# A state-space convolution's phase reduced inside its matmul, a first transform stage in 64x64 tiles, and another order of issue

## The chip, the cores and the metric

The kernel runs on one core of a Trainium2 chip. The metric is the device time of one execution in microseconds (us), median of the runs shown. A core has a matmul engine (TensorE, PE in the profile; its weight loads are PEld), three engines that work on data in SBUF and PSUM (VectorE: DVE, ScalarE: ACT, GpSimd: POOL), and a queue engine (SyncE: SP) that issues most transfers. Each engine takes its instructions in the order of the program.

## The reference

Two blocks with residuals, on one sequence of L = 2048 positions and D = 512 channels. The change lies in the first block, an S4D convolution, and in the start of the second, a gated MLP.

```python
dt = exp(log_dt);  A = -exp(log_A_real) + 1j * A_imag;  C = (C_real + 1j * C_imag) * dt[:, None]
P = exp((A * dt[:, None])[:, :, None] * pos)           # 512 channels x 128 states x 2048 positions
K = 2.0 * einsum("dn,dnl->dl", C, P).real              # a filter for each channel
y = irfft(rfft(u_t, 2 * L) * rfft(K, 2 * L), 2 * L)[:, :, :L]
h = x + (y + u * D_skip)                               # u = layernorm(x)
# second block, on layernorm(h):
z = gelu(x @ w_in);  z1 = z[..., :896];  z2 = layernorm(z[..., 896:])
out = h + (z1 * (w_sp @ z2 + b_sp)) @ w_out
```

## The kernel before

Phase A (`phase_a`) makes the filters and convolves. The position is split in two, l = 64 l1 + l2, so the filter of 16 channels is a small matmul over the 128 states of a factor W, which depends on l1, and a pair of factors E, which depends on l2. Both are a decaying amplitude times a sine or a cosine of a phase. 32 *units* make the filters of 16 channels each; 8 units are a line group c, and there are 4 groups.

A unit (`unit`) goes like this. PE makes the phases of W and E as whole and part turns: two fp32r matmuls with a stack of rows (high and low halves of three parameters for 16 channels, 96 rows, `sw`) as weights and a table `c_k` as the moving operand. ACT adds a large constant, which rounds to whole turns, and DVE subtracts this and the phase from each other, which leaves at most half a turn. ACT takes a sine of all 1024 columns, the absolute value of all 1024, and a cosine of each half of 512. POOL makes three amplitudes (`m`, 512 columns each) out of a table `mt`, DVE multiplies sines and amplitudes (`f`), and DVE and POOL the cosines. Then 16 small matmuls for the sines and 16 for the cosines (`product`) add up the filter, in four tiles of 32 columns, and it is copied to `ks`.

The transforms are done by matmuls too. `st1` is the first stage, used for the input (`piece_a`) and for the filter (`piece_c`), 32 times each: 8 matmuls of 128 rows, two tiles of 64 columns. Its moving operand `c_f` is block diagonal, four blocks of 32 rows and 32 columns for the cosines and four for the sines. `piece_b` and `piece_d` are the second stage, of input and filter, with full 128x128 weights `a2`; `piece_d` also multiplies the two spectra on DVE. `piece_e` is the inverse, in two tiles of 64 columns with `c_inv`. `evac` copies a result out of PSUM, on ACT or DVE.

PSUM is cut in two wide banks of 1024 columns and four of 512 (`WIDE`, `bank`).

The parameters come out of `params`, for group 0, for group 1, and for groups 2 and 3 together; SP writes them as rows to DRAM (`stk`, 8 transfers a group), and `stack` reads them back as `sw`. `norm_x` is the first layernorm, in two halves; `table` makes `mt`.

Phase A's order is written out by hand. The class `Plan` collects all operations; a list of ranks (RANKS) gives the place of each in the order of issue, FORMS says which of two engines takes an operation that either may take, and BANKS gives its PSUM bank. All engines, SP too, take their share of this one order. What comes after the last operation that uses a generator buffer (`cut`) is issued beside the first loads of the next phase.

`phase_b1` makes the residual, the second layernorm in four blocks of 512 positions, and the first half of the MLP's input matmul; its order is written out in the code. `lines` finishes the inverse transform, `add` adds the residual, `moments` takes statistics, `centre` and `spread` sum them over partitions by a matmul of 16 columns, `root` makes the reciprocal root, `transposed` scales and turns a block (`ht`), and `column(n, fb, w)` is the matmul of block n with columns fb, in 12 matmuls. For block 0 the first three columns are done in two halves of positions, A and B. All later phases are PE's matmuls, one after another.

## Time and profile before

| | |
|---|---|
| median of 3 runs | 839.1 us (839.03, 839.1, 842.73) |
| the profiled execution | 842.89 us |
| its span | 841.1 us |
| busy in the span: PE, DVE, ACT, POOL | 785.9 (93%), 650.9 (77%), 474.0 (56%), 300.7 (36%) us |
| mean granted clock of TensorE | 0.994 |
| phase A | 0 to 301 us; its units up to 272 us |
| phase B1 | 301 to 400 us, and the rest of the MLP up to 841 us |

Busy time counts an engine's instructions from start to end; for PE, whose matmuls overlap each other, the distance between the starts of two groups says more than the length of one. The profile's names are those of the buffers: in phase A `wa` holds `m`, `wb` holds the phases and the small constants, `trio` and `big` hold data of the transforms, `ps` is PSUM. Since all operations of phase A are issued by one helper they all have its line, L249, and are told apart by names and shapes. An fp32 matmul of the source shows as two matmuls.

### The profile page before, as it was taken

The numbers are of one execution on the slowest core, as the hardware profiler recorded it, in microseconds if no ns is written. First come the engines' busy times: TensorE is split into PE (matmuls) and PEld (weight loads), VectorE is DVE, ScalarE is ACT, GpSimd is POOL, SyncE is SP. The second block draws the span as 40 slices with busy tenths as digits, with TensorE's granted clock in tenths as the row PEclk, the third lists the DMA queues.
The fourth block names the chain that finished last, engine by engine and source line by source line (L and its number), as shares of the span: only waits on it lengthen the run. The fifth ranks groups of instructions, "written<-read, shape, count | busy, mean of one in ns | idle before, by whom it ended". The sixth has DMA issues, their size and how long they took to land.

```text
span 841.1 us, 20499 instructions
## 1 busy us (share of the span) xinstructions
PE 785.9 (93%) x8321; PEld 672.9 (80%) x8321; DVE 650.9 (77%) x1234; ACT 474.0 (56%) x795; POOL 300.7 (36%) x352
## 2 busy tenths in 40 slices
PE   0479999899999898999999999999999999999998
PEld 0278889688888898888999988888888878888887
DVE  6999999799998678663377689978856984888533
ACT  5799999789998235355223355555444443454111
POOL 5888959689877000000142100333231002232200
PEclk9999999999999999999999999999999999999999
DMA  9321613402205825445064045899799548799732
GB/s 333 95 104 41 137 40 68 113 19 53 63 3 116 327 54 138 138 138 190 36 151 125 1 150 141 186 222 222 188 209 217 152 140 202 149 249 236 166 111 77
DMA packets 64942, 115.71 MB, mean 138 GB/s; under 512 B 7024, under 2 KB 21488, under 8 KB 63952
## 3 DMA queue, kind: packets, MB, share of 16 engines
q1 hardware_dynamic: 53216, 93.04, 37.0%
q0 software_dynamic: 11632, 21.37, 15.6%
q8 instruction: 65, 1.06, 0.5%
q14 instruction: 29, 0.24, 0.1%
HBM read 86.59 MB, written 19.40 MB: 126 GB/s over the span
## 4 chain that ended last, share of the span: by engine, by line
PE 76%; DVE 11%; DMA 6%; issue 3%; ACT 2%; POOL 1%; SPq 1%; DVEq 0%; ACTq 0%; POOLq 0%
PE m L1163 26%; PE ps L249 24%; PE pz L958 9%; PE pz L852 9%; PE po L1086 5%; DVE trio L249 3%; PE pl L1086 2%; DMA zo<-scr_h 2%; DMA raws<-in_w_sp_dram 2%; DMA wa<-scr_xhat 1%; DMA trio<-in_par_dram 1%; DMA big<-in_u_a_dram 1%; DVE stats L753 1%; DVE big L249 1%; DVE wts L671 1%
## 5 line engine op out<-in xcount | busy, mean ns | idle before, releaser
L1163 PE MATMUL m<-wts,zc_wa 128*128 128x512 f32 x700 | 221.1, 395 | 0.0
L1163 PEld LDWEIGHTS m<-wts,zc_wa 128*128 128x128 f32 x700 | 131.7, 188 | 31.1 <-DVE c L1178 0.2
L1163 PE MATMUL m<-wts,zc_wb 128*128 128x512 f32 x350 | 138.1, 394 | 0.0
L1034 POOL DMA_DIRECT2D raws<-in_w_sp_dram x64 | 58.1, 971 | 212.0 <-DMA raws<-in_w_sp_dram 210.7
L249 POOL TENSOR_TENSOR wa<-mt 128x512 f32<-128x512 f32 x96 | 107.4, 1133 | 18.6 <-PE ps L249 15.4
L670 ACT CAST wts<-raws 128x512 fp32r<-128x512 f32 x112 | 69.0, 619 | 58.9 <-PE m L1163 30.7
L671 DVE TENSOR_TENSOR wts<-raws,wts 128x512 fp32r<-128x512 f32 x112 | 76.4, 684 | 20.0 <-ACT wts L670 19.9
L1163 PEld LDWEIGHTS m<-wts,zc_wb 128*128 128x128 f32 x350 | 65.8, 188 | 15.5
L958 PE MATMUL pz<-w,ht 128*128 128x448 f32 x384 | 77.0, 362 | 0.0
L958 PEld LDWEIGHTS pz<-w,ht 128*128 128x128 f32 x384 | 72.0, 187 | 4.9
L852 PE MATMUL pz<-ht,w1h 128*128 128x512 f32 (+1 forms) x248 | 74.2, 380 | 0.0
L964 POOL TENSOR_SCALAR sm<-sm 128x1 f32<-128x1 f32 x16 | 5.2, 326 | 183.5 <-DVE sm L963 183.5
L249 PEld LDWEIGHTS ps<-c_inv,trio 128*64 128x64 f32 x2048 | 63.0, 141 | 7.8 <-DVE trio L249 4.3
L249 PE MATMUL ps<-c_inv,trio 128*64 128x64 f32 x2048 | 65.4, 226 | 3.5 <-DVE trio L249 3.4
L1086 PE MATMUL po<-w,gz 128*128 128x512 f32 x252 | 61.8, 393 | 1.3 <-DVE zo L1126 1.3
L670 ACT CAST zc_wa<-raws 128x384 fp32r<-128x384 f32 (+1 forms) x70 | 36.9, 532 | 42.5 <-DVE raws L1068 25.6
L249 ACT ACTIVATE wb<-wb 128x1024 f32<-128x1024 f32 (+1 forms) x64 | 56.9, 891 | 0.9
L1086 PEld LDWEIGHTS po<-w,gz 128*128 128x128 f32 x252 | 47.3, 188 | 12.3 <-DVE zo L1126 1.7
L249 ACT ACTIVATE ps<-wb 128x1024 f32<-128x1024 f32 (+1 forms) x64 | 54.6, 859 | 3.1 <-DVE wb L249 1.3
L249 PE MATMUL ps<-big,a 128*128 128x128 f32 x448 | 54.5, 279 | 1.0 <-DVE big L249 0.9
L249 PEld LDWEIGHTS ps<-big,a 128*128 128x128 f32 x448 | 51.4, 192 | 3.5 <-issue 2.0
L852 PEld LDWEIGHTS pz<-ht,w1h 128*128 128x128 f32 x248 | 46.2, 193 | 8.8 <-ACT w1r L801 0.2
(168 smaller groups left out, 1530.0 us busy)
## 6 DMA issues: line engine op xcount, KB each, us to landing
raws<-in_w_sp_dram SPq DMA_DIRECT2D x112, 256.0 KB, 4.0
raws<-in_w_sp_dram POOLq DMA_DIRECT2D x80, 256.0 KB, 6.3
trio<-trio SPq DMA_DIRECT2D x32, 256.0 KB, 4.3
scr_z<-zo SPq DMA_DIRECT2D x28, 256.0 KB, 2.0
big<-in_u_a_dram SPq DMA_DIRECT2D x8, 512.0 KB, 7.3
xq<-in_u_b_dram SPq DMA_DIRECT2D x4, 1024.0 KB, 8.1
scr_h<-xq SPq DMA_DIRECT2D x16, 256.0 KB, 4.6
zo<-scr_z SPq DMA_DIRECT2D x14, 256.0 KB, 4.3
```

What stands on the lines that cost most here:

```text
L249: r = getattr(getattr(self.nc, e), method)(*map(self.real, args), **{k: self.real(x) for k, x in kw.items()})
L670: nc.scalar.copy(hi, src)
L671: nc.vector.tensor_sub(lo, src, hi.bitcast(F32))
L753: nc.vector.bn_stats(stats[:, n % 2, i, :], xqs[n % 3][:, i, :])
L852: nc.tensor.matmul(pt[:, w], a[:, q, f], ht[n][k][:, q, w], start=((q, i) == terms[0]), stop=((q, i) == terms[-1]))
L958: nc.tensor.matmul(pt[:, :FQ], a[:, q], w2[:, b, q, f], start=(q == 0 and i == 0), stop=(q == 3 and i == 2))
L964: nc.gpsimd.tensor_scalar_add(sm[:, 14:15], sm[:, 13:14], 1e-5)
L1034: nc.gpsimd.dma_start(r, ws[1], accum_op=ALU.add)
L1086: nc.tensor.matmul(pt, gz[fb][x][:, P * a:P * a + P], wo[:, y, fb, w], start=(first and fb == fbs[0] and i == 0), stop=(last and fb == fbs ...
L1163: nc.tensor.matmul(pt, x[:, f], y, start=(k == 0 and i == 0), stop=(k == KT - 1 and i == 2))
```

## The change

- The phase matmul now leaves at most half a turn by itself. The stack has 16 rows for each of 8 channels instead of 6 for each of 16 (128 rows, two weight sets `sw[:, 0]` and `sw[:, 1]` for a unit instead of one): the six parameter rows, four rows of ones, and the six parameter rows once more. The table `c_k` has for these the values, a quarter turn, the large constant, its negative, minus a quarter turn, and the negated values. So the sum over the rows is rounded where the constant comes in and the phase is subtracted behind it. The rows of ones are written to DRAM by two transfers (`marks`), the parameter rows by two transfers for each one of before.
- ACT's rounding and DVE's subtraction of each unit go.
- In the first 8 units (`TURNED`) there are two pairs of phase matmuls, one for W and one for E, each with and without a quarter turn. One ACT sine of 1024 columns for each gives sine and cosine; there is no absolute value and no cosine pass, and one DVE multiplication of 1024 columns weighs both halves of W. In the other 24 units there is one pair, the absolute value is read from PSUM, and sine and cosines are as before; the weight multiplication of the cosine may be on POOL or DVE.
- `st1` is done in four 64x64 tiles: 16 matmuls of 64 rows with 64 moving columns, without the half of `c_f` that holds only zeros. Its result lies in a wide bank, one half for the upper rows and one for the lower.
- PSUM: three wide banks and two others.
- RANKS, FORMS and BANKS are new throughout. FORMS now puts 83 of the transforms' 128 evacuations on ACT and 45 on DVE (61 and 67 before) and 3 of the 24 weight multiplications on DVE.
- In `phase_b1` the three B columns of block 0 come ahead of `centre(1)`, column 3 ahead of `root(1)`, columns 4 and 5 into `transposed(1)`, and column 6 behind it.

The diff without the three lists and without renamed views:

```diff
-WIDE = 2
+WIDE = 3
 SUC = 8
+TURNED = 8
...
-    ck = np.zeros((6, 16, 2, 16, 32))
-    for i in range(16):
-        j = 4 * (i % 4) + i // 4
-        ck[:2, i, 0, j, :] = 1.0
-        ck[2:4, i, 0, j, :] = l1
-        ck[4:, i, 1, j, :] = np.arange(32) + 0.5
-    c["c_k"] = ck.reshape(96, 1024)
+    ck = np.zeros((8, 16, 2, 2, 8, 32))
+    for i in range(8):
+        a = ck[i, :, :, :, i]
+        for r, sign in ((0, 1.0), (10, -1.0)):
+            a[r + 0, :, 0] = a[r + 3, :, 0] = sign * l1
+            a[r + 1, :, 0] = a[r + 4, :, 0] = sign
+            a[r + 2, :, 1] = a[r + 5, :, 1] = sign * (np.arange(32) + 0.5)
+        a[6, 1], a[7], a[8], a[9, 1] = 0.25, MAGIC, -MAGIC, -0.25
+    c["c_k"] = ck.reshape(P, 1024)
+    c["c_one"] = np.ones((1, 4 * 4 * NS))
...
-    cs_bufs = [wb(2 * W).rearrange("p (i w) -> p i w", i=2) for _ in range(3)]
+    cs_bufs = [wb(2 * W).rearrange("p (k a w) -> p k a w", k=2, a=2) for _ in range(2)]
...
-    rcs = one(g1, "rcs", [NCH, 2, NS])
-    sws = [one(g1, f"sw{h}", [4, NS]) for h in range(2)]
+    rcs = wb(NCH * 2 * NS).rearrange("p (c i s) -> p c i s", c=NCH, i=2)
+    sws = [one(g1, f"sw{h}", [2, 4, NS]) for h in range(2)]
...
-    nc.gpsimd.dma_start(c_k[:96], cst["c_k"].rearrange("p (i w) -> p i w", i=2))
+    nc.gpsimd.dma_start(c_k, cst["c_k"].rearrange("p (i w) -> p i w", i=2))
+    marks = stk_d.rearrange("c h (i r) s n -> (c h i) (r s n)", r=16)[:, 6 * 4 * NS:10 * 4 * NS]
+    for w in (slice(0, 32), slice(32, 128)):
+        nc.sync.dma_start(marks[w], cst["c_one"].to_broadcast([w.stop - w.start, 16 * NS]))
...
-            d = stk_d[c0 + c]
             for su in range(SUC):
-                nc.sync.dma_start(d[su // 4].rearrange("(k i) s n -> s i k n", k=6)[su % 4], st6[16 * su:16 * su + 16, :, c, :])
+                d = stk_d[c0 + c, su // 4].rearrange("(i r) s n -> s i r n", r=16)[su % 4]
+                for r in (0, 10):
+                    nc.sync.dma_start(d[:, r:r + 6], st6[16 * su:16 * su + 16, :, c, :])
...
-        nc.sync.dma_start(sws[h][:96], stk_d[c, h])
+        nc.sync.dma_start(sws[h], stk_d[c, h].rearrange("(a p) s n -> p a s n", a=2))
...
-        sw, f3, cs, m = sws[s // 4][:96, s % 4, :].bitcast(F32R), f_bufs[su % 3], cs_bufs[su % 3], m_bufs[su % 2]
-        ph = nc.bank([P, 2, W], 2)
-        with nc.group():
-            for i in range(2):
-                nc.tensor.matmul(ph[:, i, :], sw, c_k[:96, i, :], start=True, stop=True)
-        nc.scalar.activation(cs, ph, AF.Identity, bias=magic)
-        nc.vector.scalar_tensor_tensor(cs, cs, MAGIC, ph, op0=ALU.subtract, op1=ALU.subtract)
-
-        ph = nc.bank([P, 2, W], 2)
-        nc.scalar.activation(ph, cs, AF.Sin, scale=-TWO_PI)
-        sn = ph[:, 1, :]
-        nc.scalar.activation(cs, cs, AF.Abs)
-        ce, cw = nc.bank([P, 1, W], 0), cs[:, 0, :]
-        nc.scalar.activation(ce, cs[:, 1:2, :], AF.Sin, bias=half_pi, scale=-TWO_PI)
-        nc.scalar.activation(cw, cs[:, 0, :], AF.Sin, bias=half_pi, scale=-TWO_PI)
+        sw, f, m = sws[s // 4][:, :, s % 4].bitcast(F32R), f_bufs[su % 3], m_bufs[su % 2]
+
+        cv = c_k.rearrange("p k (i w) -> p i k w", i=2)
+
+        def phases(c):
+            ph = nc.bank([P, 2, W], 2)
+            with nc.group():
+                for ab in range(2):
+                    nc.tensor.matmul(ph[:, ab, :].rearrange("p (k w) -> p k w", k=2), sw[:, ab], c, start=True, stop=True)
+            return ph, ph.rearrange("p a (k w) -> p a k w", k=2)
+
         mt = mts[s // 4]
         d0 = 16 * (s % 4)
         for i, (a0, b0) in ((2, (18, 30)), (0, (3, 26)), (1, (11, 0))):
             ta = mt[:, d0:d0 + 16, a0:a0 + 8].unsqueeze(2).to_broadcast([P, 16, 4, 8])
             tb = mt[:, d0:d0 + 16, b0:b0 + 4].unsqueeze(3).to_broadcast([P, 16, 4, 8])
             nc.gpsimd.tensor_tensor(m[:, i, :].rearrange("p (d b a) -> p d b a", d=16, a=8), tb, ta, op=ALU.mult)
-
-        nc.vector.tensor_mul(f3[:, 0, :], ph[:, 0, :], m[:, 2, :])
-        nc.vector.scalar_tensor_tensor(f3[:, 1, :], m[:, 0, :], -1.0, sn, op0=ALU.mult, op1=ALU.mult)
-        nc.vector.tensor_mul(f3[:, 2, :], sn, m[:, 1, :])
+        mv = m.rearrange("p i (a w) -> p i a w", a=2)
+        fw = f[:, 0:2].rearrange("p i w -> p (i w)").rearrange("p (a k w) -> p a k w", a=2, k=2)
+        fe = f[:, 2:4].rearrange("p i (a w) -> p i a w", a=2)
+
+        if su < TURNED:
+            flat, ph = phases(cv[:, 0])
+            nc.scalar.activation(flat, flat, AF.Sin, scale=-TWO_PI)
+            nc.vector.tensor_mul(fw, ph, mv[:, 2].unsqueeze(2).to_broadcast([P, 2, 2, W // 2]))
+            flat, ph = phases(cv[:, 1])
+            nc.scalar.activation(flat, flat, AF.Sin, scale=-TWO_PI)
+            sn, ce, wt = ph[:, :, 0], ph[:, :, 1], fw[:, :, 1]
+        else:
+            cs = cs_bufs[su % 2]
+            flat, ph = phases(c_k[:, 0].rearrange("p (i w) -> p i w", i=2))
+            nc.scalar.activation(cs, ph.rearrange("p a k w -> p k a w"), AF.Abs)
+            nc.scalar.activation(flat, flat, AF.Sin, scale=-TWO_PI)
+            sn, wt, ce = ph[:, :, 1], cs[:, 0], nc.bank([P, 2, W // 2], 0)
+            nc.scalar.activation(ce, cs[:, 1], AF.Sin, bias=half_pi, scale=-TWO_PI)
+            nc.scalar.activation(wt, wt, AF.Sin, bias=half_pi, scale=-TWO_PI)
+            nc.vector.tensor_mul(fw[:, :, 0], ph[:, :, 0], mv[:, 2])
+            nc.either(lambda: nc.gpsimd.tensor_tensor(wt, wt, mv[:, 2], op=ALU.mult), lambda: nc.vector.tensor_mul(wt, wt, mv[:, 2]))
+        nc.vector.scalar_tensor_tensor(fe[:, 0], mv[:, 0], -1.0, sn, op0=ALU.mult, op1=ALU.mult)
+        nc.vector.tensor_mul(fe[:, 1], sn, mv[:, 1])
         kp = nc.bank([P, 4, 2, 32], 0)
 
-        def product(wt, et, i):
-            for dd in range(4):
-                for q in range(4):
-                    o = (4 * dd + q) * 32
-                    nc.tensor.matmul(kp[32 * q:32 * q + 32, dd, :, :], wt[:, o:o + 32], et[:, :, o:o + 32],
-                                     start=(i == 0 and dd == 0), stop=(i == 1 and dd == 3), tile_position=(0, 32 * q))
-
-        with nc.group():
-            product(f3[:, 0, :], f3[:, 1:3, :], 0)
-        nc.vector.tensor_mul(m[:, 0:2, :], ce.to_broadcast([P, 2, W]), m[:, 0:2, :])
-        nc.gpsimd.tensor_tensor(cw, cw, m[:, 2, :], op=ALU.mult)
-        with nc.group():
-            product(cw, m[:, 0:2, :], 1)
+        def product(k, wt, et):
+            with nc.group():
+                for dd in range(4):
+                    for q in range(4):
+                        i = 4 * q + dd
+                        w = wt[:, i // 8, 32 * (i % 8):32 * (i % 8) + 32]
+                        nc.tensor.matmul(kp[32 * q:32 * q + 32, dd, :, :], w, et[:, :, 32 * i:32 * i + 32],
+                                         start=(k == 0 and dd == 0), stop=(k == 1 and dd == 3), tile_position=(0, 32 * q))
+
+        product(0, fw[:, :, 0], f[:, 2:4])
+        nc.vector.tensor_mul(mv[:, 0:2], ce.unsqueeze(1).to_broadcast([P, 2, 2, W // 2]), mv[:, 0:2])
+        product(1, wt, m[:, 0:2])
...
     def st1(src):
-        pt = bank("s1", [P, 4, 4, NK1])
+        pt = nc.bank([P, 2, W], 2).rearrange("p h (q x) -> p (h q) x", q=2)[:, :, :4 * NK1].rearrange("p q (d k) -> p q d k", d=4)
         with nc.group():
             for dd in range(4):
-                for ri in range(2):
-                    nc.tensor.matmul(pt[64 * ri:64 * ri + 64, dd, :, :], src[:, dd, :],
-                                     c_f[:, P * ri:P * ri + P], start=True, stop=True, tile_position=(0, 64 * ri))
+                for h in range(2):
+                    for ri in range(2):
+                        r, o = slice(64 * h, 64 * h + 64), P * ri + 64 * h
+                        nc.tensor.matmul(pt[64 * ri:64 * ri + 64, 2 * h:2 * h + 2, dd, :], src[r, dd, :], c_f[r, o:o + 64],
+                                         start=True, stop=True, tile_position=(64 * h, 64 * ri))
         return pt
...
-        evac(x1us[c > 0][:, :, 4 * s:4 * s + 4, :].rearrange("p k d q -> p k (d q)"), pt.rearrange("p d q k -> p k (d q)"))
+        evac(x1us[c > 0][:, :, 4 * s:4 * s + 4, :], pt.rearrange("p q d k -> p k d q"))
...
-        evac(x1k[:, :, :, 4 * s:4 * s + 4], pt.rearrange("p d q k -> p k q d"))
+        evac(x1k[:, :, :, 4 * s:4 * s + 4], pt.rearrange("p q d k -> p k q d"))
...
-        column(0, 0, B)
+        for fb in range(3):
+            column(0, fb, B)
         centre(1)
-        column(0, 1, B)
         add(2, 0)
+        add(2, 1)
+        column(0, 3)
         root(1, spread(1))
-        column(0, 2, B)
-        transposed(1, [((column, 0, 3),), (), ((column, 0, 4),), ()])
-        for fb in range(5, 7):
-            column(0, fb)
-        for g in range(1, 4):
+        transposed(1, [((column, 0, 4),), (), ((column, 0, 5),), ()])
+        column(0, 6)
+        for g in range(2, 4):
```

## Rows read from the trace of the kernel before

**Rows 1.** Stages: length, busy time of PE, PEld, DVE, ACT, POOL (instructions), clock, DMA, GB/s

```profile
45.00:272.00 227.00, 218.31 (x5099) 195.32 (x5101) 214.49 (x292) 210.20 (x284) 185.82 (x199) 0.99 0.29 69
301.00:331.00 30.00, 26.83 (x349) 25.85 (x345) 23.44 (x82) 14.94 (x28) 0.00 (x0) 0.94 0.51 117
331.00:841.00 510.00, 505.06 (x2261) 420.19 (x2260) 358.94 (x694) 213.04 (x413) 83.50 (x112) 1.00 0.63 158
```

**Rows 2.** Timeline of PE: start us, length us, line, operation, out<-in, shapes, count

```profile
129.18 0.65 PE L249 MATMUL ps<-f 128*32 128x64 f32 x32
129.65 0.63 PE L249 MATMUL ps<-wa,wb 128*32 128x64 f32 x32
130.21 0.73 PE L249 MATMUL ps<-c_k,sw 96*128 96x512 f32 x2
130.88 3.95 PE L249 MATMUL ps<-c_inv,trio 128*64 128x64 f32 x128
134.76 0.65 PE L249 MATMUL ps<-f 128*32 128x64 f32 x32
...
210.13 2.84 PE L249 MATMUL ps<-wb,ks 128*64 128x128 f32 x48
212.90 1.16 PE L249 MATMUL ps<-big,a 128*128 128x128 f32 x8
```

**Rows 3.** Groups, 45 to 272 us: names, shapes, count | busy us, mean ns | idle before

```profile
L249 DVE TENSOR_TENSOR f<-ps,wa 128x512 f32<-128x512 f32 x64 | 42.9, 681 | 0.4 <-ACT ps L249 0.2
L249 POOL TENSOR_TENSOR wb<-wb,wa 128x512 f32<-128x512 f32 x32 | 41.1, 1285 | 13.1 <-ACT wb L249 12.9
L249 DVE TENSOR_TENSOR wa<-ps,wa 128x1024 f32<-128x1024 f32 x32 | 38.8, 1214 | 2.8 <-ACT ps L249 2.5
L249 DVE SCALAR_TENSOR_TENSOR wb<-wb,ps 128x1024 f32<-128x1024 f32 x30 | 36.2, 1213 | 2.4 <-ACT wb L249 2.1
L249 ACT ACTIVATE wb<-wb 128x1024 f32<-128x1024 f32 x32 | 33.9, 1058 | 0.5
...
L249 ACT ACTIVATE ps<-wb 128x1024 f32<-128x1024 f32 x32 | 32.9, 1029 | 2.1 <-DVE wb L249 1.3 <-DVE trio L249 0.3 <-DVE f L249 0.2
L249 ACT ACTIVATE wb<-ps,wb 128x1024 f32<-128x1024 f32 x29 | 31.9, 1111 | 2.3 <-PE ps L249 1.6 <-issue 0.4 <-POOL wa L249 0.2
...
L249 DVE COPY big<-ps 128x512 f32<-128x512 f32 x37 | 25.1, 682 | 3.5 <-PE ps L249 3.3
L249 ACT COPY big<-ps 128x512 f32<-128x512 f32 x41 | 23.5, 582 | 7.5 <-PE ps L249 7.2
L249 ACT ACTIVATE wb<-wb 128x512 f32<-128x512 f32 x32 | 23.1, 723 | 0.4
L249 ACT ACTIVATE ps<-wb 128x512 f32<-128x512 f32 x32 | 22.0, 689 | 1.0 <-DVE big L249 0.7
L249 DVE SCALAR_TENSOR_TENSOR f<-wa,ps 128x512 f32<-128x512 f32 x32 | 21.6, 676 | 0.2 <-ACT ps L249 0.2
```

**Rows 4.** Timelines of SP, DVE and PE around the start of the transforms

```profile
26.71 3.66 SPq L249 DMA_DIRECT2D scr_stk<-trio  x8
...
43.73 1.22 DVE L249 TENSOR_TENSOR big<-big,ps 128x1024 f32<-128x1024 f32 x1
...
45.01 8.63 PE L249 MATMUL ps<-wb,big 128*64 128x128 f32 x112 [5.30 <-DVE big L249]
```

**Rows 5.** Timelines of PE and DVE in the second layernorm, block 1

```profile
323.10 0.28 PE L852 MATMUL pz<-ht,w1l 128*128 128x256 f32 x1
323.22 0.28 PE L852 MATMUL pz<-ht,w1h 128*128 128x256 f32 x1
325.90 0.80 PE L762 MATMUL lnh_pm<-stats,c_mean 128*128 128x16 f32 x4 [2.40 <-DVE stats L753]
...
329.98 0.17 DVE L781 TENSOR_SCALAR small<-lnh_pv 128x16 f32<-128x16 f32 x1 [1.87 <-PE lnh_pv L776]
...
338.50 0.69 DVE L814 TENSOR_TENSOR ht<-w1r,ht 128x512 fp32r<-128x512 f32 x1 [0.17 <-ACT ht L810]
```

## What the change does to the time: the prediction

> **What bounds the kernel now.** I read the stages first, then the tensor engine's own sequence, then the prices of the other engines' instructions. The profiled execution took 842.89 us, of which its span is 841.1; the three timed runs have a median of 839.1, so the profiled one is 3.8 us above it, and I carry a difference in microseconds from the one to the other.
>
> The stages [rows 1] show the same bound nearly everywhere: PE is busy 218.3 of 227 us from 45 to 272 and 505.1 of 510 us from 331 to the end. The change touches only what lies before 345 us or so. Behind that PE has no room, so what is won or lost in front of it moves the end by as much.
>
> In the stage 45 to 272 (the units and the transforms beside them) PE is not alone: DVE is busy 214.5 us, ACT 210.2, POOL 185.8 of 227. Three engines at 93 to 96% mean that taking work from one of them alone gives nearly nothing. A gain needs PE, DVE and ACT to become lighter together.
>
> A busy PE is not a PE at its peak, so I take PE prices from the starts of consecutive groups [rows 2]. Every fp32 matmul in the source shows as two passes. A first-stage piece (8 source matmuls, 16 passes of 128 columns into two 64-column tiles) takes (212.90 - 210.13)/3 = 0.92 us in a run of three; many stand alone between groups of other tilings, so I use 0.94. A unit's two products (32 passes of 64 columns each, four tiles of 32 columns) take 0.47 and 0.56 us, so 0.52. The inverse (64 columns, two tiles) takes (134.76 - 130.88)/128 = 30 ns a pass, so 0.97 for 32 passes. A unit's pair of phase matmuls takes 130.88 - 130.21 = 0.67.
>
> **The change part by part: PE.** The new first stage has 16 source matmuls a piece, so 32 passes of 64 columns, in four 64x64 tiles: half the streamed columns, since the blocks of zeros in c_f are skipped. No row of before has a matmul that starts at partition 64 of its operands, so the price is bounded from both sides. The product group has the same 32 passes, the same 64 columns and four tiles at once: 0.52. The inverse has the same 64-column weights, but two tiles at once: 0.97, which would be a loss of 0.03 a piece. I take 0.52. In the inverse each of the two tiles spends 61 ns a pass with a 64-column load in it, so such a load hides behind a pass of 64 columns; and the products show four tiles at work at one time. What no row shows is two of them above each other. 64 pieces x (0.94 - 0.52) = -26.9 us; the bounds are -26.9 and +1.9.
>
> The Trainium skill's page "TensorE: Matmul & The Clock Gate" (Measured speedup vs the span model) has four row tiles at 3.07 times one tile, not 4. By it a piece, as an estimate, would take 0.52 x 4/3.07 = 0.68 us and the gain would be 17 us. The products here show no such loss for tiles beside each other; for tiles above each other no row shows it.
>
> Units 0 to 7 make their phase twice over (once for the W half, once for the E half, each with and without the quarter turn), two phase pairs instead of one: 8 x 0.67 = +5.4 us. Contraction over 128 rows instead of 96 streams the same 512 columns, so I cost it at nothing.
>
> **The other engines.** DVE loses the subtraction of the rounded phase, 1.21 us in all 32 units [rows 3]. In units 0 to 7 the 0.68 multiplication becomes one of 1024 elements (1.21). Units: 32 x 4.47 = 142.9 before; 8 x 3.79 + 24 x 3.25 = 108.3 after, and 3 weight multiplications that the form list gives to DVE (2.0). The form list also moves 22 of DVE's 67 transform evacuations to ACT: -15.0 for DVE, +12.8 for ACT. DVE: about -48 in the whole phase. ACT loses the rounding pass (1.11) everywhere, and in units 0 to 7 the absolute value and both half cosines too (they become sines in the 1024 wide passes): 32 x 4.61 = 147.5 before, 8 x 2.06 + 24 x 3.50 = 100.5 after, so -47 + 12.8 + 4 of smaller copies = -30. POOL loses 11 weight multiplications at 1.29 and some normalisations: -17.
>
> So the stage of 227 us would hold DVE 166, ACT 180, POOL 169 and a PE with 22 us less. None of the three is above PE. That cover is why I cost their edits at nothing on the path: PE alone sets the length. If PE did not become lighter, their 48, 30 and 17 us would bring at most the 8.7 us that PE idles in that stage.
>
> **The start.** PE's first-stage work begins at 45.01, released by DVE's last normalisation add (43.73, 1.22 long) [rows 4]. I read the order lists out of the diff and summed DVE's instructions ahead of that add, at the durations of this trace: 44.6 us before, 46.7 after. Two roundings (2.4) leave; unit 0's three multiplications (2.6) and the second parameter set's first steps come. In the new order the first piece also stands behind unit 0's products, which need one more wide multiplication (1.21) and 0.5 us of PE: it starts at about 48.8, so +3.8. But PE then has 1.1 us more of its list behind it, so +2.7 in all. The bounds: 0 (DVE reaches the add no later) and +6 (the stack is late). The parameter writes to the stack double: for each line group 16 instead of 8, at (from 26.71, 8 issues, 3.66 long) 0.46 each on SP [rows 4], so 3.7 us later. Queued behind them on SP are the loads of sw. Unit 0's phase is listed behind the second normalisation's statistics, near 41 us, where sw would come at some 35: about 6 us of cover remain. Later sets write 48 more of these, 22 us of SP spread over units 3 to 13, with the loads of xt, the exchange and the next sw behind them on SP. By the lists SP has 21 us of issues in the 53 us from unit 7 to unit 15; I cost that at nothing. The two fills with ones go once, before the stack is read.
>
> **The reordered block behind the transforms.** PE stops after the third A column (323.22, the last of passes 0.12 apart) until 325.90, waiting for DVE's moments [rows 5], and the stage 301 to 331 has a granted clock of 0.94 [rows 1], so about 3.6 us at the lower level (1.2 GHz). Now the three B columns come first: 36 x 0.12 = 4.3, to 327.7, by which time the moments are done (PE took them up at 325.90). Mean 0.5, column 3 12 x 0.235 = 2.8, variance 0.5: 331.5. DVE then needs, as before, from 329.98 to 339.19 = 9.2 us for the root and the turning: 340.7. PE has only columns 4 to 6 left to hide it, 8.4 us, so 339.9: a new wait of 0.8. Column 0 of the second block starts at 340.7. Before: 329.9 (just ahead of DVE's 329.98) + 1.4 + 4 x 2.8 = 342.5. So -1.8, between -4.3 (no new wait, no lower clock) and +1.
>
> **Sum.** -26.9 + 5.4 + 2.7 - 1.8 = -20.6 us: 842.9 becomes 822.3 for the profiled execution, and 839.1 becomes 818.5 for the median. PE's 8.7 us of idle in the stage are kept in this; if the lighter engines remove them, 809.8.
>
> **The rivals.**
> *Another engine or the banks take PE's place.* By the lists, from unit 7's end to unit 15's end PE has 53 us, POOL 55, DVE 50, ACT 47 and its table loads: no slack between them. Also the banks go from two wide and four narrow to three wide and two narrow: five groups in flight instead of six, and each first-stage piece now holds a wide one, whose evacuation (0.58 on ACT, 0.68 on DVE [rows 3]) is longer than the piece. For it: the four sums. Against it: before, the stretch 102 to 168 had PE at 62 of 66 us with three engines about as close. Price: half the 20.6, so 828.8. The Trainium skill's "TensorEngine Tiling (Array Packing)" (PSUM Bottleneck) says that tiling speeds the matmul and not the evacuation, which then can bound; the copies' rows agree that they are the longer part.
>
> *The four tiles overlap only in part.* Then a piece takes what a product group lasts from its first start to its last end, 0.65 us [rows 2]: 64 x 0.29 = -18.6, sum -12.3: 826.8. By the skill's 3.07 the piece would be near this.
>
> *Tiles above each other don't run at the same time: slower.* The mechanism is one: 32 passes go at the two-tile price of the inverse, 0.97. Then +1.9 + 5.4 + 2.7 - 1.8 = +8.2: 847.3. It decides from a piece price of 0.94 - 6.3/64 = 0.84 us on. For it: no row shows it otherwise. Against it: the products' four tiles.
>
> *More than forecast.* The idle goes too: 809.8.
>
> **How the numbers follow.** Forecast 0.50 (own range 812 to 825), more 0.07, another bound 0.18, partial overlap 0.13, slower 0.12. The range 807 to 838 leaves out the slower case and little else. Half a per cent, about what a measurement of this kernel can tell from no change, is 4.2 us. Faster than 834.9: 0.50 + 0.07 + 0.13 + 0.10 of the other bound = 0.80. Within: 0.08, from the worse half of that rival. Slower: 0.12.
>
> **What would show it.** Right: in the timeline of PE, starts of first-stage pieces in a run 0.5 to 0.56 apart; the last product near 252 instead of 271; the first y matmul near 282 instead of 301.87; DVE busy about 48 us less; no wait of PE between the A columns and the statistics' matmul. Wrong: pieces 0.9 us apart (the slower rival); pieces at 0.5 but PE idle of over 15 us in the units' stage, with waits on POOL, ACT or bank readers (the first rival); a first piece later than 51 us (the start).

## The result: slower by half a per cent, and the profile after

The changed kernel takes 842.4 us (median) beside 839.1 of the kernel before on the same chip: ratio 1.005, 95% interval 1.003 to 1.007. The forecast was 818.5. So the change is slower by 3.3 us where 20.6 us less were expected. The profiled execution of after took 841.5 us (span 839.7), the one of before 842.9 (841.1).

The stages of after, as in [rows 1] (start and end, length, then busy us of PE, PEld, DVE, ACT, POOL with their instructions, TensorE's granted clock, DMA share, GB/s):

```profile
45.00:272.00 227.00, 202.77 (x6020) 179.66 (x6013) 167.46 (x227) 173.76 (x258) 171.87 (x187) 0.97 0.34 86
...
301.00:331.00 30.00, 29.24 (x484) 28.39 (x479) 24.23 (x76) 16.93 (x31) 0.00 (x0) 1.00 0.40 93
```

DVE holds 167 us of the first stage instead of 214, ACT 174 instead of 210, POOL 172 instead of 186, near the prediction's 166, 180 and 169. But PE has about 920 more matmul passes there (a pass is one matmul record with its weight load), is busy 15.5 us less, and nothing comes earlier: the first y matmul starts at 305.8 us instead of 301.87. PE now stands idle for 24 of 227 us, where it stood idle for 9.

What PE waits for up to 305 us (waiting tile and line, what released it: us in all, times, longest). First after, then before:

```profile
PE ps L253 <- issue: 21.6, 18, 3.2
```

```profile
PE ps L249 <- DVE trio L249: 23.2, 7, 11.8
PE ps L249 <- DVE big L249: 6.2, 2, 5.3
...
PE ps L249 <- DMA wa<-scr_xhat: 3.4, 2, 3.2
...
PE ps L249 <- POOL wb L249: 2.0, 3, 1.5
```

"Issue" is idle time in which nothing that the profile shows was awaited. Before has no such wait in this view; after has 18, 21.6 us in all, the largest entry of the view (the next is DVE trio, 16.5). The timeline of PE in after shows where they fall (start us, length us, line, operation, out<-in, shapes, count, idle before and its releaser):

```profile
78.94 0.69 PE L253 MATMUL ps<-wb,ks 64*64 64x64 f32 x32
79.56 0.65 PE L253 MATMUL ps<-wa,f 128*32 128x64 f32 x32
...
80.66 0.65 PE L253 MATMUL ps<-wb,ks 64*64 64x64 f32 x32
81.13 0.28 PE L253 MATMUL ps<-wb,big 64*64 64x64 f32 x4
84.11 1.01 PE L253 MATMUL ps<-wb,big 64*64 64x64 f32 x27 [2.69 <-issue]
...
90.66 0.28 PE L253 MATMUL ps<-wb,ks 64*64 64x64 f32 x3
92.46 2.08 PE L253 MATMUL ps<-wb,ks 64*64 64x64 f32 x125 [1.53 <-issue]
94.41 0.33 PE L253 MATMUL ps<-wb,big 64*64 64x64 f32 x3
96.34 0.68 PE L253 MATMUL ps<-wb,big 64*64 64x64 f32 x29 [1.60 <-issue]
...
216.50 1.63 PE L253 MATMUL ps<-wb,ks 64*64 64x64 f32 x96
217.94 0.69 PE L253 MATMUL ps<-wb,wa 64*64 64x64 f32 x32
218.46 0.41 PE L253 MATMUL ps<-wb,ks 64*64 64x64 f32 x10
221.29 0.57 PE L253 MATMUL ps<-wb,ks 64*64 64x64 f32 x22 [2.42 <-issue]
```

Two things are to be seen. The price of a piece is what was forecast: three take 217.94 - 216.50 = 1.44 us, 0.48 each; one is 0.47 after the next (80.66 to 81.13) or 0.62 when a group of another form follows (78.94 to 79.56). And the stalls shown here fall in the middle of a piece, after 4, 3 or 10 of its 32 passes, where its data and its bank had already been granted. Between two of them lie 125 + 3 = 128 matmul records (92.46 to 96.34). With its weight load each record is two instructions of PE, so 256.

The page of after counts the transfers that bring instructions (queue, kind: packets, MB, share):

```profile
q8 instruction: 73, 1.20, 0.6%
```

PE has 9361 matmuls and 9361 weight loads: 18722 instructions in 73 packets are 256 to a packet, 16 KB each. Before, with 1040 matmuls less, there were 65 packets. That this queue (q8) brings PE's instructions is read from these counts. So the theory was: the stalls are PE waiting for its own instructions. A first-stage piece now has twice the passes, each of half the columns (32 of 64 instead of 16 of 128; what the four tiles halve is the columns that each of them streams), and in a row of short groups PE runs through a packet faster than the next one comes.

### The profile page after: what moved, and what is told of

It is laid out like the page before. It is cut to its first block, busy times and chain, and to the rows that moved or that the text cites. A ratio compares the mean times of both kernels' runs of the same rounds, so it can differ in the third digit from the quotient of the medians.

```text
span 839.7 us, 22552 instructions
## 1 busy us (share of the span) xinstructions
PE 770.3 (92%) x9361; PEld 657.0 (78%) x9361; DVE 603.3 (72%) x1172; ACT 441.6 (53%) x778; POOL 285.1 (34%) x339
## 4 chain that ended last, share of the span: by engine, by line
PE 63%; DVE 1%; ACT 1%; issue 0%
PE m L1186 33%; PE pz L981 9%; PE pz L875 8%; PE po L1109 7%; PE pl L1109 2%; PE ps L253 2%; PE y L757 1%; DVE stats L776 0%; ACT w1r L824 0%; DVE xq L772 0%; ACT ht L833 0%; PE lnh_pm L785 0%; PE lnh_pv L799 0%; ACT zo L878 0%; ACT big L253 0%
## 5 line engine op out<-in xcount | busy, mean ns | idle before, releaser
L693 ACT CAST wts<-raws 128x512 fp32r<-128x512 f32 x112 | 69.0, 619 | 47.6 <-DMA raws<-in_w_sp_dram 21.1
L253 PE MATMUL ps<-c_inv,trio 128*64 128x64 f32 x2048 | 63.4, 224 | 3.2 <-DVE trio L253 2.2
L253 PE MATMUL ps<-big,a 128*128 128x128 f32 x448 | 56.1, 286 | 1.7 <-DVE trio L253 1.0
L253 PEld LDWEIGHTS ps<-big,a 128*128 128x128 f32 x448 | 54.5, 200 | 3.6 <-DVE trio L253 1.3
L1109 PEld LDWEIGHTS po<-w,gz 128*128 128x128 f32 x252 | 47.3, 188 | 10.7
L253 DVE TENSOR_TENSOR f<-ps,wa 128x512 f32<-128x512 f32 (+1 forms) x64 | 46.8, 750 | 8.6 <-ACT ps L253 4.1
L253 DVE COPY big<-ps 128x512 f32<-128x512 f32 x39 | 26.1, 687 | 30.9 <-PE ps L253 30.8
```

Of the source, the lines that this page charges most:

```text
L253: r = getattr(getattr(self.nc, e), method)(*map(self.real, args), **{k: self.real(x) for k, x in kw.items()})
L693: nc.scalar.copy(hi, src)
L1109: nc.tensor.matmul(pt, gz[fb][x][:, P * a:P * a + P], wo[:, y, fb, w], start=(first and fb == fbs[0] and i == 0), stop=(last and fb == fbs ...
```

## The experiments

Theory A throughout: PE is held up by the supply of its instructions. The rivals are named in each expectation.

**1. Matmuls alone.** A kernel in which no engine but PE works between its first loads and its end; it stores zeros and computes nothing of the reference. Its body:

```
rest(40)
for forms in ("4", "2", "42", "i", "4"):   # 64x64 tiles, 128x64 tiles, in turn, inverse, 64x64
    for i in range(24): group(forms[i % len(forms)])
    rest(30)                               # 512-column matmuls
```

> A kernel of its own with no other engine at work: five stretches of 24 groups of matmuls with nothing to wait for, between long 512-column matmuls: (1) the new first-stage group in 64x64 tiles (16 matmuls, 64 instructions), (2) the old group in 128x64 tiles (8 matmuls, 32 instructions), (3) the two in turn, (4) a group in the form of the inverse (32 matmuls, 128 instructions), (5) as (1). Theory A, the limit is the supply of TensorE's instructions (packets of 256 that follow each other 3.3 to 4.0 us apart in the trace of after): stretches 1 and 5 take 17 to 24 us each instead of 24 x 0.52 = 12.5, with idle time put to issue in the middle of groups; stretch 2 takes 22.6 (24 x 0.94) without such idle time; stretch 3 about 17.5 to 19 (12 x 1.46, hardly held up); stretch 4 about 46 (24 x 1.92). Theory B, the stalls come from the kernel around it (a bank, an engine, a transfer): stretches 1 and 5 take 12.5, stretch 3 17.5, no idle time put to issue anywhere.

The timeline of PE, with the first stretch, the second, a pair of the third, the fourth and the start of the last:

```profile
41.64 4.19 PE L138 MATMUL pw<-c_f,src 64*64 64x64 f32 x271
46.82 2.09 PE L138 MATMUL pw<-c_f,src 64*64 64x64 f32 x128 [0.99 <-issue]
50.55 2.09 PE L138 MATMUL pw<-c_f,src 64*64 64x64 f32 x128 [1.64 <-issue]
54.27 2.09 PE L138 MATMUL pw<-c_f,src 64*64 64x64 f32 x128 [1.64 <-issue]
58.28 1.90 PE L138 MATMUL pw<-c_f,src 64*64 64x64 f32 x113 [1.91 <-issue]
60.11 26.02 PE L130 MATMUL po<-wide,c_f 128*128 128x512 f32 x60
86.06 21.18 PE L145 MATMUL pw<-c_f,src 128*64 128x128 f32 x384
...
133.11 0.69 PE L138 MATMUL pw<-c_f,src 64*64 64x64 f32 x32
...
134.76 0.69 PE L138 MATMUL pw<-c_f,src 64*64 64x64 f32 x32
...
178.85 45.02 PE L154 MATMUL pi<-c_f,src 128*64 128x64 f32 x1536
...
249.75 3.49 PE L138 MATMUL pw<-c_f,src 64*64 64x64 f32 x223
```

With nothing else at work the same stalls are there. The bursts of exactly 128 records start 3.73 us apart (46.82, 50.55, 54.27; the one behind them 4.01, and in the last stretch 3.45 to 3.73), so the supply is some 3.73/128 = 29.1 ns a pass, while the passes themselves take 2.09/128 = 16.3 ns. The stretch lasts 60.11 - 41.64 = 18.5 us, not 12.5, and the last one 270.13 - 249.75 = 20.4. The old form (21.1 us, 0.88 a group) and the inverse (45.0 us, 29.3 ns a pass) run without a stall. Theory B is out. One thing was not foreseen: in turn, a pair takes 134.76 - 133.11 = 1.65 us instead of 0.52 + 0.88 = 1.40 (19.8 us for the stretch instead of 17.5), with no idle time shown. Each change of form costs some 0.12 us.

The trace's records of transfers show the packets themselves. In the last stretch PE resumes at 262.01, the next packet of q8 starts 1.12 us later (263.13), lands at 264.40, and PE resumes 1.34 us behind that, at 265.74. In after it is the same: each of the 18 stalls ends 1.2 to 1.6 us after a packet of q8 has landed (82.66 and 84.11, 91.10 and 92.46, 273.77 and 275.26). This shows the mechanism in the changed kernel itself.

**2. The old first stage inside after.** All 64 pieces in two tiles, the order of issue and all else as in after:

```
-  for h in range(2): matmul(pt[64*ri:.., 2*h:2*h+2, dd, :], src[64*h:.., dd, :], c_f[64*h:.., o:o+64], tile_position=(64*h, 64*ri))
+  matmul(pt[64*ri:.., :, dd, :], src[:, dd, :], c_f[:, P*ri:P*ri+P], tile_position=(0, 64*ri))
```

The edit is shortened here; the result lies in one half of the same wide bank.

> After, with all 64 first-stage pieces in the old two-tile form (8 matmuls instead of 16), everything else and the order of issue as in after. Theory A, supply of instructions: the pieces cost 0.94 instead of 0.52 (+26.9 us of matmul), but the 21.6 us of idle time put to issue fall below 6 and the granted clock of 45 to 272 comes back from 0.97 to near 1.00, so that the time is 838 to 848, within about 1% of before. Theory B, the idle time has another cause in the new order (a bank, a transfer): it stays, and the time is 842.4 + 26.9 = 869. Rival C, the order of issue alone is what loses the gain: the time is above 850 with the waits moved to semaphores of DVE, ACT or POOL.

834.2 us, ratio to before 0.9948 (0.9936 to 0.9960), faster than the expected 838 to 848. The waits for issue fall to one:

```profile
PE ps L253 <- issue: 1.2, 1, 1.2
```

So a first stage with 20 us more of busy PE makes the kernel 8 us faster. B and C are out: the waits went, none came in their place, and the same order of issue is now faster than before. The groups of PE between 45 and 300 us show where after loses (names, shapes, count | busy us, mean ns | idle before), first after:

```profile
L253 PE MATMUL ps<-big,a 128*128 128x128 f32 x448 | 56.1, 286 | 1.7 <-DVE trio L253 1.0 <-ACT big L253 0.7
...
L253 PE MATMUL ps<-wb,ks 64*64 64x64 f32 x1024 | 23.3, 230 | 10.2 <-issue 9.4 <-ACT big L253 0.8
...
L253 PE MATMUL ps<-wb,big 64*64 64x64 f32 x512 | 12.9, 240 | 6.0 <-issue 5.0 <-DVE wa L253 0.6 <-ACT trio L253 0.4
L253 PE MATMUL ps<-wb,wa 64*64 64x64 f32 x512 | 10.6, 222 | 1.2 <-ACT wb L253 0.8 <-DVE f L253 0.4
```

and the run with the old form:

```profile
L253 PE MATMUL ps<-big,a 128*128 128x128 f32 x448 | 53.7, 278 | 1.7 <-DVE trio L253 1.0 <-ACT big L253 0.7
L253 PE MATMUL ps<-wb,ks 128*64 128x128 f32 x512 | 32.8, 274 | 0.8 <-ACT big L253 0.8
...
L253 PE MATMUL ps<-wb,big 128*64 128x128 f32 x256 | 17.6, 285 | 0.9 <-ACT trio L253 0.8 <-DVE wa L253 0.2
L253 PE MATMUL ps<-wb,wa 128*64 128x128 f32 x256 | 16.8, 274 | 0.7 <-DMA wa<-scr_xhat 0.7
```

The first stage is 46.8 us instead of 67.2, so 20.4 us less; against it stand 20.4 us more of idle time put to issue, and groups that the change of form doesn't touch are dearer (ps<-big,a 56.1 beside 53.7), at a granted clock of 0.97 beside 1.00 in the stage from 45 to 272.

**3. Every second piece in the old form** (`old = s % 2 == 0`).

> After, with every second first-stage piece (even ones) in the old two-tile form. Matmul work grows by 32 x 0.42 = 13.4 us against after. Theory A, supply of instructions: a pair of pieces holds 48 matmul passes in 1.46 us, 30 ns each, about what the supply allows, so the idle time put to issue falls from 21.6 to under 8 and the clock recovers: the time is 830 to 840, below after by 2 to 12 us although there is more to compute. Theory B, another cause: 842.4 + 13.4 = 856, the idle time as in after.

828.2 us, ratio 0.9875 (0.9857 to 0.9893), and in a second run on another occasion 829.8, 0.9884 (0.9859 to 0.9909). It beats both kernels: 10 us faster than before, 14 faster than after, though 32 of its pieces are the dearer ones. The waits for issue are 3.6 us and 2.6. The measured time is below the expected 830 to 840.

> The kernel with every second piece in the old form once more, beside the chosen mix on the same chip: 826 to 831 as before.

**4. The old tiles, cut in two.** The same two tiles and as many columns as in experiment 2, but as many instructions as in the new form:

```
-  matmul(pt[64*ri:.., :, dd, :], src[:, dd, :], c_f[:, P*ri:P*ri+P], tile_position=(0, 64*ri))
+  for h in range(2): matmul(pt[64*ri:.., 2*h:2*h+2, dd, :], src[:, dd, :], c_f[:, o:o+64], tile_position=(0, 64*ri))
```

> After with the first-stage pieces in the old 128x64 tiles, but each matmul cut into two of 64 columns: the same two tiles and the same columns in all as in the run with the old form everywhere (834.2 us), and as many instructions as the new 64x64 form (64 instead of 32 a piece). Theory A, supply of instructions: a piece of 32 passes needs 32 x 29.1 ns = 0.93 us of supply, as much as it takes to run, so it leaves nothing for the 128x32 products beside it, which run at 15 ns a pass: idle time put to issue between the 1.2 us of the old form and the 21.6 of the new, 4 to 14 us, and a time of 837 to 848. Theory B, it is the 64x64 tiles themselves that stall TensorE: no new idle time, 834.2 within 1.5 us.

844.5 us, ratio 1.007 (1.0053 to 1.0087): 10 us slower than the uncut form.

```profile
PE ps L253 <- issue: 6.8, 11, 1.5
```

Cutting alone, with no 64x64 tile in the kernel, brings the stalls back (1.2 to 6.8 us). Theory B, that these tiles stall PE, is out. The cut itself costs too: in experiment 1 the inverse, with the same shapes, takes 32 x 29.3 = 0.94 us for 32 passes where the uncut group takes 0.88, so some 3.7 us in 64 pieces.

**5. One kind of piece in the old form**: those of the spectra of x, or those of the kernels.

> After with the 32 first-stage pieces of the spectra of x (from big and wa) in the old form and the 32 of the kernels (from ks) in 64x64 tiles. The same number of pieces of each form as in the run where every second piece is old (828.2). Theory A, supply of instructions: what counts is how the short passes bunch. In the last channel (210 to 275 us) there are no pieces of x, and the kernels' pieces stand directly beside the products, so the stalls of after there (8.3 us between 221 and 275) stay and those before 100 us (6.5 us) go: idle time put to issue 8 to 13 us, time 831 to 837. Theory B, only the number of pieces in each form counts: 3.6 us and 828.2 within 1.5.

> After with the 32 first-stage pieces of the kernels (from ks) in the old form and the 32 of the spectra of x in 64x64 tiles. Theory A: the last channel, which has no pieces of x, no longer stalls; what stays is some of the 6.5 us before 100 us: idle time put to issue 3 to 8 us, time 827 to 833, below the run with the old form for x alone. Theory B, only the number of pieces in each form counts: as the run with every second piece old, 828.2 within 1.5.

841.6 us (1.0028; 1.0009 to 1.0046) with the pieces of x in the old form, 830.6 (0.9900; 0.9881 to 0.9919) with those of the kernels. Both have 32 pieces in either form, as experiment 3; the waits for issue are 11.2, 3.4 and 3.6 us. So not the number but how the pieces bunch counts, as theory A has it. But 841.6, with the pieces of x in the old form, is above its 831 to 837, and one stall that should have gone is its longest (3.1 us, ending at 95.33). How much of this the busy DMA engines beside its stalls account for isn't separated here. Windows of that run, in the columns of the stages:

```profile
266.00:270.00 4.00, 3.11 (x118) 2.75 (x108) 2.84 (x4) 2.27 (x4) 1.49 (x2) 0.68 1.01 211
270.00:276.00 6.00, 3.21 (x103) 2.85 (x102) 0.00 (x0) 1.77 (x4) 0.21 (x1) 0.50 0.81 250
276.00:282.00 6.00, 5.68 (x30) 5.68 (x31) 2.45 (x2) 0.27 (x1) 0.00 (x0) 0.57 1.02 421
```

Around a stall of 2.5 us (it ends at 272.4) TensorE has the lower level of its clock (1.2 GHz) for much of 16 us. Busy time times what the clock lacks: 3.11 x 0.32 + 3.21 x 0.50 + 5.68 x 0.43 = 5.0 us. My expectation had counted the idle time alone.

**6. A mix chosen piece by piece.** 27 pieces in the old form, picked with a model of the supply fixed at 3.73 us a packet.

> After with 27 of the 64 first-stage pieces in the old two-tile form and 37 in 64x64 tiles, chosen piece by piece so that nowhere in the order of issue do the matmul passes come faster than the supply seen in the kernel of matmuls alone (a packet of 256 instructions each 3.73 us, with some 150 passes in hand), and so that neighbours keep the same form (a pair of unlike groups took 1.65 us there, two like ones 1.04 and 1.77). Theory A, supply of instructions: idle time put to issue under 4 us and a clock as in the run with every second piece old, with 5 more pieces in the short form and fewer changes of form: about 4 us below that run, 820 to 828. Theory B, only the number of pieces in each form counts: not below that run by more than its own scatter, 826 to 830.

837.5 us (0.9969; 0.9949 to 0.9989): a miss, well above both expectations, with 9.8 us of waits for issue. More short pieces than in experiment 3 were not better, and the fixed 3.73 us was not enough to place them. The two longest stalls behind 200 us (2.2 us ending at 217.6, 1.9 at 269.8) lie in stretches where the DMA engines are busy 79 and 102% (a third, of 2.0 us, ends at 94.77, at a share of 0.47 from 91.8 to 95.8):

```profile
215.00:218.00 3.00, 0.81 (x42) 0.59 (x32) 0.34 (x1) 2.74 (x4) 2.81 (x3) 1.00 0.79 201
267.00:270.00 3.00, 1.12 (x66) 0.89 (x59) 0.00 (x0) 1.10 (x3) 0.21 (x1) 1.00 1.02 340
```

**7. How long a burst may be.** Matmuls alone again (zeros stored), bursts of n groups with 4.3 us of long matmuls between.

> Matmuls alone: six times a burst of n groups in 64x64 tiles (32 passes each at 16 ns) and then 5 long matmuls (4.3 us), for n = 2, 4, 6, 8 and 10. If a packet of 256 instructions takes 3.73 us and about 150 passes are in hand when the next is asked for, bursts of 2 and 4 groups (64 and 128 passes) run without idle time, 6 (192) have at most one or two stalls in the six, and 8 and 10 (256 and 320) stall by 1 to 1.7 us in nearly every burst. If the limit were the mean rate alone (29 ns a pass over burst and gap), 8 and below would not stall: 266 passes in 8.5 us are 32 ns each.

Bursts of 2 and 4 groups (64 and 128 passes) never stall; of six bursts of 6 groups two do (behind a third PE stalls after one long matmul, 0.67 us), of 8 groups four, of 10 groups all six. From the timeline of PE, a burst for n = 4, for n = 6 and for n = 8:

```profile
101.36 2.09 PE L138 MATMUL pw<-c_f,src 64*64 64x64 f32 x128
...
166.19 2.55 PE L138 MATMUL pw<-c_f,src 64*64 64x64 f32 x159
170.01 0.73 PE L138 MATMUL pw<-c_f,src 64*64 64x64 f32 x33 [1.26 <-issue]
...
260.35 3.96 PE L138 MATMUL pw<-c_f,src 64*64 64x64 f32 x256
```

Some 155 to 270 passes go before PE runs dry (155 at the least here, 271 in experiment 1); that this depends on where in a packet the burst begins would fit, but isn't shown. The mean rate doesn't decide: bursts of 8 stall although burst and gap together give 32 ns a pass.

**8. Transfers beside it.** Experiment 1 with loads of data from the start, first on one queue (DMA engines 27% busy in the first stretch), then in rows of 512 bytes on two queues.

> The kernel of matmuls alone, with 24 loads of 1 MB on SyncE's queue from its start (about 100 us of transfers), so that the first stretches run beside them and the last (250 us) does not. If a packet of instructions has to wait behind data, the first stretch of 24 groups in 64x64 tiles takes more than the 18.5 us that it took with idle queues (idle time between bursts of 128 matmul records above the 1.64 us seen there), and the stretch of the old form more than 21.2. If not, both are as without the loads within 0.5 us.

> The kernel of matmuls alone once more, with 16 loads of 1 MB in rows of 512 bytes on each of two queues from its start, so that the 16 DMA engines are far busier beside the first stretches than the 27% of the run with loads before (in the changed kernel the share stands at 0.85 to 0.97 from 81 to 94 us, and single stalls last up to 3.2 us there instead of 1.64). If a packet of instructions waits behind data once the DMA engines are full, the bursts of 128 in the first stretch lie more than 3.73 us apart, the idle time before them goes to 2 to 3 us and the stretch from 18.5 to 20 to 26 us. If the length of the kernel's stalls has another cause, 1.64 and 18.5 as before.

At 27% nothing changes (bursts 3.45 to 3.73 us apart; the old form takes 21.2 us as before). With the DMA engines full:

```profile
55.10 3.69 PE L140 MATMUL pw<-c_f,src 64*64 64x64 f32 x128 [5.47 <-issue]
62.67 3.69 PE L140 MATMUL pw<-c_f,src 64*64 64x64 f32 x128 [3.88 <-issue]
...
228.85 2.09 PE L140 MATMUL pw<-c_f,src 64*64 64x64 f32 x128 [0.87 <-issue]
```

the packets come 7.57 us apart instead of 3.73, and the first stretch takes 80.61 - 45.02 = 35.6 us instead of 18.5 (above the expected 20 to 26). A packet itself still takes 1.2 us, but it starts 4.8 us after PE resumes instead of 1.1. The passes between the stalls take 3.69 us for 128 instead of 2.09; that is the clock, which was granted at half there (columns as before, without ACT):

```profile
55.10:58.80 3.70, 3.69 (x128) 3.50 (x128) 0.00 (x0) 0.00 (x0) 0.50 1.20 290
```

The first burst, at 47.54, still had the full clock and took 2.09 us beside the same transfers (share 1.19); the next came 7.56 us later all the same. So the supply, not the clock, sets the distance. The last stretch of the same run, with idle queues, is as in experiment 1.

**9. The new order behind the transforms, alone, in before.**

```
-  column(0, 0, B); centre(1); column(0, 1, B); add(2, 0); root(1, spread(1)); column(0, 2, B)
-  transposed(1, [((column, 0, 3),), (), ((column, 0, 4),), ()])
+  column(0, 0, B); column(0, 1, B); column(0, 2, B); centre(1); add(2, 0); add(2, 1); column(0, 3); root(1, spread(1))
+  transposed(1, [((column, 0, 4),), (), ((column, 0, 5),), ()])
```

> Before, with only the new order of the first lines of the second stage's start (three column products, then the sum of group 1, then the scale and the transposes). Theory: this part of the change is worth what the two traces show from the first column product to the end, 539.2 against 533.9, so 839.1 - 5.3 = 834 (between 833.5 and 837.5, the latter by the sum of the prediction, -1.8). Rival: the shorter tail of after came from what its first part left further ahead, and the time is 839.1 within 1.

835.7 us, ratio 0.9969 (0.9956 to 0.9982): faster by 2.9 us (1.5 to 3.7). The rival is out.

## Why the prediction was wrong, step by step

**The step that failed** is the first-stage term, -26.9 us, "64 pieces x (0.94 - 0.52)". Its price for the new piece was right: 0.47 to 0.62 us in after, 18.5 us less 6 us of stalls for 24 in experiment 1, so the rivals with dearer tiles fell. The old piece was put somewhat too high (0.88 in experiment 1, where the term has 0.94). But the term took the price of a single group of 32 passes [rows 2] for the price of 64 of them. In before such a group (a product) stood alone or in pairs between longer ones; the change puts pieces of the same kind between them, five groups in a row from 78.94 on. Experiment 2 measures the term with everything else in place: 842.4 - 834.2 = +8.2 us, 35 us from the forecast. Between 45.7 us and the first y matmul, at 305.8 in after and at 297.8 with the old form, PE is busy 13.8 us less and idle 21.8 us more. The busy time would be about 20 us less (46.8 beside 67.2 in the first stage); some 6 go to the lower clock, 202.8 us at 0.97 instead of 1.00. Experiments 1, 4 and 7 show that the idle time is the supply of instructions. Experiment 8 offers a reason why single stalls grow to 3.2 us: in after the three longest (2.4, 2.7 and 3.2 us) stand where the DMA engines are busy (share 0.97, 0.96 and 0.87 below). And behind five of the six of 1.6 us and more the clock falls: to 0.50 from 149 to 151 us behind the stall that ends at 146.77, and also around those that end at 84.11, 96.34, 163.90 and 275.26, but not around the one that ends at 221.29:

```profile
84.00:89.00 5.00, 4.22 (x161) 3.80 (x163) 2.60 (x5) 1.54 (x3) 1.36 (x1) 0.71 0.97 260
...
149.00:151.00 2.00, 2.00 (x50) 1.83 (x40) 1.48 (x4) 1.97 (x4) 1.64 (x3) 0.50 0.00 0
218.00:222.00 4.00, 1.58 (x88) 1.37 (x82) 1.91 (x3) 1.48 (x3) 1.51 (x2) 1.00 0.96 228
271.00:276.00 5.00, 1.82 (x89) 1.64 (x89) 1.15 (x1) 0.87 (x2) 1.24 (x1) 0.87 0.87 274
```

**What could have been read beforehand.** The trace of before has the size of a packet: 8321 matmuls in 65 packets, so 128 to a packet. How close two packets can follow each other it doesn't show: the old first stage (58 ns a pass) and the inverse (30 ns) [rows 2] don't ask for them faster than they came in experiment 1, and the products (15 ns) stand only 64 passes together.

The Trainium skill's page "Runtime: NRT & Kernel Launch" (Instruction fetch mechanics) says that the instructions come in blocks of 256 and that the cost of crossing into the next is mostly hidden. The first half agrees with the trace (73 packets for 18722 instructions). The second doesn't hold here: 21.6 us in after, and in experiment 1 the blocks of short passes cost 1.4 to 1.9 us each.

**The other terms** were forecast at +6.3 us together (+5.4, +2.7, -1.8) and measured at 834.2 - 838.6 = -4.4 (experiment 2, against before on the same chip): 10.7 us better. So the whole miss is 35.1 - 10.7 = 24.4 us (842.4 - 818.5 = 23.9 by the medians; the kernel before was at 838.6 beside experiment 2, and at 839.1 beside after).

- The phase pair in units 0 to 7, +5.4: the size was right. The group ps<-c_k,sw goes from 20.1 to 25.2 us in the run with the old first stage. Contraction over 128 rows costs nothing, as said: in after a pair takes 52.84 - 52.17 = 0.67 us, as before.
- The start, +2.7: wrong in size. The first piece starts at 45.77, not at 48.8, hardly later than before [rows 4].
- The other engines "costed at nothing": wrong in the kernel's favour. Their cuts were sized well (DVE 47 us, ACT 36, POOL 14 less in the stage 45 to 272). But PE had been waiting for some of it. With the old first stage its waits on POOL wb (2.0 us in before) go to 0.2 and those on DMA wa from 3.4 to 0.7, while those on ACT big and ACT trio rise from 0.2 to 3.5. (Most of before's wait on DVE big, 5.3 of 6.2 us, ends at 45.01, ahead of the first piece, which comes no earlier now.) From 45.7 us to the first y matmul PE idles 10.2 us instead of 13.2. The rival "more than forecast" had this mechanism. The idle time accounts for 3 us; PE's busy time there is 1 us less than before (241.9 beside 242.9) where 5 more were due, of which the granted clock (1.00 instead of 0.99 in 45 to 272) could be 2. The rest stays open.
- The block behind the transforms, -1.8: right in direction, measured at -2.9 alone (experiment 9). PE no longer stops ahead of the statistics, as the timeline of after shows (the last column product starts at 329.99, and no idle time stands in the row):

```profile
330.11 0.51 PE L785 MATMUL lnh_pm<-stats,c_mean 128*128 128x16 f32 x4
```

  and the clock of that stage is 1.00 instead of 0.94 [rows 1].

**The signs that I had named** say it partly: pieces 0.5 us apart, DVE about 48 us lighter and no wait between the A columns and the statistics' matmul came true; the last product is at 275.38 instead of 252, the first y matmul at 305.8 instead of 282. "PE idle of over 15 us in the units' stage" came true as well, but I had put it to waits on POOL, ACT or the readers of banks, and it was none of them. The rival that ended slower (a piece at 0.97) had a near time, 847, by luck: its reason, tiles that don't run at the same time, isn't there.

**What stays open.** Why the three parts of a packet's 3.4 to 3.7 us (in experiment 1's last stretch 1.1 us from PE's start to the packet's, 0.9 to 1.3 of transfer, 1.3 to 1.5 to PE's next start) take as long as they do isn't shown. That full DMA engines lengthen it is shown for matmuls alone, in one run; in the kernel it is read from the DMA share beside the stalls, and no run took the transfers away there. It isn't doubled there throughout: the bursts of after that start at 84.11, 88.48 and 92.46 are 4.4 and 4.0 us apart at a share of 0.98. At 143 to 147 us after has a stall of 1.9 us at a share of 0.12, so they don't explain every one beyond 1.64. A mix better than experiment 3's was tried once and failed.

## What to carry to other kernels

Ahead of cutting matmuls into more and smaller tiles, count TensorE's instructions as well as its columns: a sustained stretch of short passes did not go below about 29 ns a pass (a matmul and its weight load) in experiment 1, and not below 59 ns beside the two queues of loads in experiment 8, although a pass alone takes 16.3. What counts is the bunching: 128 short passes in a row ran freely, 256 mostly not. Where short groups must stand together, leave some in the longer form or put long matmuls between them; here half of the pieces in the old form gave 828 us, better than either form for all.

## What the runs showed of the hardware

- TensorE's instructions come in packets of 256 (16 KB), 3.4 to 4.0 us apart with idle queues, 7.6 us beside two queues of loads in rows of 512 bytes (DMA share 1.2); PE first ran dry 155 to 270 passes into a burst. A stall ends 1.2 to 1.6 us after a packet has landed. In a trace the stall shows as idle time put to issue mostly in the middle of a group, with 128 matmul records or a multiple between two stalls.
- Four 64x64 tiles, two of them above each other, run at 16.3 ns a pass, the price of the four tiles of 32 columns beside each other (0.47 to 0.56 us for 32 [rows 2]). No loss for tiles above each other shows.
- A change between two tilings costs about 0.12 us (1.65 us for an unlike pair instead of 1.40).
- Behind five of after's six stalls of 1.6 us and more TensorE's clock falls to its lower level (1.2 GHz, granted 0.50), so that such a stall costs more than its own length. It stays at 1.00 around the sixth (2.4 us, at 221 us) and through the stalls of 1.64 us in experiment 1; beside the stalls of 3.9 to 5.5 us in experiment 8 it falls.
